# A gated recurrence and a SwiGLU layer on one core: the main path reordered as a list schedule, with smaller first units, narrower weight conversion, on-chip moves and another form of the output product

## The chip, the cores and the metric

The kernel runs on one core of a Trainium2 chip. A core has five engines with a queue each: PE (matrix products; the loads of its stationary operands are listed as PEld), DVE and ACT (elementwise work, ACT also functions from tables that have to be loaded), POOL (elementwise work and DMAs), and SP, which here only starts DMAs. Every queue runs in order. The metric is the device time of one launch in microseconds.

## The reference

For 4 x 8 heads of width D = 48 and 768 steps, a complex state is decayed by a gate and read out by q; the outputs of all heads are one row of 384 features for a feed-forward layer of width 1536.

```python
mag = np.sqrt(a_re * a_re + a_im * a_im)
scale = np.minimum(mag, 0.999) / (mag + 1e-06)
a_re_n, a_im_n = (a_re * scale, a_im * scale)
for t in range(S):
    new_re = ar * S_re - ai * S_im          # ar, ai: row t of a_re_n, a_im_n
    new_im = ar * S_im + ai * S_re
    S_re, S_im = (new_re + kv, new_im)      # kv: outer product of k and v, row t
    y[:, :, t] = np.einsum('bhd,bhde->bhe', q[:, :, t], S_re)
...
xn = x / rms * rms_g                        # x: y as (3072, 384)
silu = g * (1.0 / (1.0 + np.exp(-g)))       # g = xn @ w_gate
return (silu * (xn @ w_val) @ w_out).astype(np.float32)
```

The three weight matrices arrive as float64 and are converted to float32 ("narrowed") in the kernel; [...]this is done on pairs of 32-bit words.

## The kernel before

Time is cut into 24 chunks of C = 128 steps, six to a batch. Inside a chunk the recurrence is a masked product of all pairs of rows plus one product with the state at the chunk's start. For this the decays are turned into a magnitude and an angle per feature and step, accumulated over the chunk, and put into k and q as rotations: every row of k and q becomes a cosine and a sine part.

`fast` (L472) is the path that runs. `general` (L46) stands in the program behind a flag, `bad`, for inputs outside the range that `fast` handles.

- **Gates** (`load_gates` L514, `gates` L560): one call works on a unit of UC = 2 chunks, 768 elements in each of 128 partitions (three blocks j of features by 256 steps). ACT computes squares, inverse roots, arctangent and sines; DVE does products and the running products and sums (scans, L592 and L612). The results go to `rot`, 12 rows of 129 elements per chunk.
- **The move** (L626 to L634): `rot` has (head, feature) on the partitions and the products need the feature alone there. Each chunk is written to `way` in DRAM by one DMA (L629), and read back as `kq` by another (L631), both on SP.
- **Scores** (`scores` L712): 8 heads of k by q into `s_ps`, DVE multiplies by the causal mask into `am` (L723), PE transposes k for the state (L732), ACT copies it to `kt`.
- **Finish** (`finish` L736): the state is updated (L744, DVE); `y_ps` sums, per head, `am` by v (L755) and q by the state (L757), with 48 output columns and the 128 steps on the partitions. ACT squares y and sums its rows (L761), POOL takes the power -1/2 (L765), ACT scales, PE transposes three blocks (L774), DVE multiplies by the norm's weights into `xT` (L775).
- **Feed-forward** (`feed_forward` L780): a group is GC = 3 chunks. For each of 12 blocks of 128 hidden features: gate and value products (L792, 384 moving columns), Silu on ACT (L795), their product on DVE to `hT`; then three output products (L803) and a copy and a store each.
- **Weights** (`load_weights` L682, `narrow` L662): 18 pieces of 768 KB are fetched on SP and narrowed by one ACT operation, two `tensor_scalar` and four two-input DVE operations of 768 elements each. Five fetches are issued at the start, and narrowing goes on between the chunks.

The order is given by Python generators: the loop at the end of `fast` runs `scores(n)` and `finish(n - 1)`, and between their parts pulls pieces of the feed-forward of the group before (`filler`) and of the next unit's gates (`ahead`). In these listings `tt` is DVE's `tensor_tensor`, `stt` its `scalar_tensor_tensor` (both have lines L501 and L504 in the profile).

Of the kernel before, what the change touches and what calls it, by code (L numbers as in the profile page):

```python
# [16 lines left out]
P = 128  # L29
C = 128  # L30
# [440 lines left out]

def fast(tc, ctx, qT, kT, v, a_re, a_im, w_gate, w_val, w_out, rms_g, out, H, bad):  # L472
# [10 lines left out]
    GC = 3  # L483
    NG = N // GC
    GT = GC * C
    UC = 2
    T = UC * C
    NU = N // UC
    L = P // H
    assert NCH % GC == 0 and NCH % UC == 0 and DM % P == 0 and D2 <= P and L * ND == D  # L490

    consts = ctx.enter_context(tc.tile_pool(name="consts", bufs=1))
    prep = ctx.enter_context(tc.tile_pool(name="prep", bufs=1))
    unit = ctx.enter_context(tc.tile_pool(name="unit", bufs=2))
    act = ctx.enter_context(tc.tile_pool(name="act", bufs=2))
    dram = ctx.enter_context(tc.tile_pool(name="dram", bufs=2, space=DRAM))
    ps_a = ctx.enter_context(tc.tile_pool(name="ps_a", bufs=4, space=PSUM))
    ps_g = ctx.enter_context(tc.tile_pool(name="ps_g", bufs=4, space=PSUM))

    def tt(o, x, y, op=ALU.mult):  # L500
        nc.vector.tensor_tensor(out=o, in0=x, in1=y, op=op)  # L501

    def stt(o, x, c, y, op0, op1=ALU.mult, **kw):
        nc.vector.scalar_tensor_tensor(out=o, in0=x, scalar=c, in1=y, op0=op0, op1=op1, **kw)  # L504
# [6 lines left out]
    UN = [dict() for _ in range(NU)]  # L511
    U = [dict() for _ in range(N)]

    def load_gates(u):  # L514
        b, c = divmod(u * UC, NCH)
        t = UN[u]
        for name, ap in (("re", a_re), ("im", a_im)):
            t[name] = prep.tile([P, ND, T], FP32, tag=name, name=name, bufs=2)
            rows = ap[b].rearrange("(h j l) s -> j l h s", j=ND, l=L)
            queue = nc.scalar if u == 0 and name == "im" else nc.sync  # L520
            for j in range(ND):
                queue.dma_start(out=t[name][:, j], in_=rows[j][:, :, c * C:c * C + T])
        for name, ap in (("k", kT), ("q", qT)):
            t[name] = prep.tile([P, ND, T], FP32, tag=name, name=name)
            for i in range(UC):
                nc.sync.dma_start(
                    out=t[name][:, :, i * C:(i + 1) * C],
                    in_=ap[u * UC + i].rearrange("d (h t) -> (d h) t", t=C)
                                      .rearrange("(j p) t -> p j t", p=P))
        for n in range(u * UC, (u + 1) * UC):  # L530
            U[n]["v"] = unit.tile([C, H, D], FP32, tag="v", name="v", bufs=4)
            nc.sync.dma_start(out=U[n]["v"].rearrange("t h d -> t (h d)"),
                              in_=v[n * C:(n + 1) * C, :])
# [3 lines left out]
    rot = consts.tile([P, 4 * ND, UC, C + 1], FP32, name="rot")  # L537
    nc.vector.memset(rot[:, :, :, C:], 0.0)
    load_gates(0)

    zeros = consts.tile([P, T], FP32, name="zeros")
    nc.gpsimd.memset(zeros, 0.0)
    starts = consts.tile([P, ND, UC, C], FP32, name="starts")
    nc.gpsimd.memset(starts, 0.0)
    halfpi = consts.tile([P, 1], FP32, name="halfpi")
    nc.gpsimd.memset(halfpi, PI / 2)
    round_ = consts.tile([P, 1], FP32, name="round_")
    nc.gpsimd.memset(round_, ROUND)
    cap = consts.tile([P, 1], FP32, name="cap")
    nc.gpsimd.memset(cap, CAP)  # L550
    mid = consts.tile([P, 1], FP32, name="mid")
    nc.gpsimd.memset(mid, -(RE_MAX + RE_MIN) / 2)
    width = consts.tile([P, 1], FP32, name="width")
    nc.gpsimd.memset(width, -(RE_MAX - RE_MIN) / 2)
    nc.scalar.activation(out=width, in_=width, func=AF.Abs_reciprocal_sqrt)
    nc.gpsimd.memset(width, -(RE_MAX - RE_MIN) / 2)
    ends = consts.tile([P, NU, ND, UC], FP32, name="ends")
    range_ = consts.tile([P, NU], FP32, name="range_")

    def gates(u):  # L560
        t = UN[u]
        re, im, q, k = (t[x] for x in ("re", "im", "q", "k"))
        act_ = nc.scalar.activation

        s, w, y, r, p = (prep.tile([P, ND, T], FP32, tag=x, name=x)
                         for x in ("s", "w", "y", "r", "p"))
        act_(out=s, in_=re, func=AF.Square)
        act_(out=w, in_=im, func=AF.Square)
        tt(s, s, w, ALU.add)
        act_(out=y, in_=re, func=AF.Abs_reciprocal_sqrt)  # L570
        act_(out=y, in_=y, func=AF.Square)
        act_(out=r, in_=s, func=AF.Abs_reciprocal_sqrt)
        act_(out=w, in_=re, func=AF.Abs, bias=mid)
        act_(out=w, in_=w, func=AF.Relu, bias=width, accum_out=range_[:, u:u + 1])

        tt(im, im, y)
        tt(re, re, y)
        stt(im, re, 2.0, im, ALU.subtract, reverse0=True)
        yield

        tt(w, s, r)
        stt(s, w, -0.5, r, ALU.mult)
        stt(w, s, 1.5, w, ALU.add)

        act_(out=r, in_=r, func=AF.Identity, scale=-CAP * EPS_MAG, bias=cap)
        stt(w, w, EPS_MAG, r, ALU.subtract, ALU.min)

        by_chunk = lambda x: x.rearrange("p j (c t) -> p j c t", t=C)
        wc = by_chunk(w)
        nc.vector.tensor_copy(out=starts[:, :, :, 0:1], in_=wc[:, :, :, 0:1])  # L590
        nc.vector.memset(wc[:, :, :, 0:1], 0.0)
        nc.vector.tensor_tensor_scan(out=flat(p), data0=flat(w),  # L592
                                     data1=starts.rearrange("p j c t -> p (j c t)"),
                                     initial=0.0, op0=ALU.mult, op1=ALU.add)
        nc.vector.tensor_copy(out=ends[:, u], in_=p.rearrange("p j (c t) -> p j c t", t=C)[:, :, :, C - 1])
        nc.vector.tensor_copy(
            out=rot[:, 2 * ND:, :, C].rearrange("p (a j) c -> p a j c", j=ND),
            in_=ends[:, u].unsqueeze(1).to_broadcast([P, 2, ND, UC]))
        yield
        act_(out=r, in_=p, func=AF.Abs_reciprocal_sqrt)  # L600
        act_(out=r, in_=r, func=AF.Square)
        act_(out=im, in_=im, func=AF.Arctan)
        act_(out=im, in_=im, func=AF.Copy, scale=0.5 / PI)

        tt(s, p, r)
        stt(r, s, 2.0, r, ALU.subtract, reverse0=True)
        tt(k, k, r)
        tt(q, q, p)
        yield

        for j in range(ND):
            nc.vector.tensor_tensor_scan(  # L612
                out=re[:, j], data0=im[:, j], data1=zeros, op0=ALU.add, op1=ALU.add,
                initial=UN[u - 1]["turn"][:, j] if u * UC % NCH else 0.0)
        act_(out=w, in_=re, func=AF.Identity, bias=round_)
        stt(im, w, ROUND, re, ALU.subtract, ALU.add, reverse0=True)
        turn = t["turn"] = prep.tile([P, ND, 1], FP32, tag="turn", name="turn", bufs=2)
        nc.vector.tensor_copy(out=turn, in_=im[:, :, T - 1:T])
        act_(out=w, in_=im, func=AF.Abs)
        act_(out=s, in_=im, func=AF.Sin, scale=2 * PI)  # L620
        act_(out=y, in_=w, func=AF.Sin, scale=-2 * PI, bias=halfpi)
        yield
        for i, (x, f) in enumerate(((k, y), (k, s), (q, y), (q, s))):
            tt(rot[:, i * ND:(i + 1) * ND, :, 0:C], by_chunk(x), by_chunk(f))
        yield
        for i in range(UC):  # L626
            n = u * UC + i
            way = dram.tile([4 * DM, C + 1], FP32, tag="way", name="way")
            nc.sync.dma_start(out=way.rearrange("(r p) t -> p r t", p=P), in_=rot[:, :, i])  # L629
            to = unit.tile([D2, 2, H, C + 1], FP32, tag="kq", name="kq", bufs=3)  # L630
            nc.sync.dma_start(out=to.rearrange("d x h t -> d x (h t)"),  # L631
                              in_=way.rearrange("(x d h) t -> d x (h t)", x=2, h=H))
            U[n]["k"], U[n]["q"] = to[:, 0, :, 0:C], to[:, 1, :, 0:C]
            U[n]["decay"] = to[:, 1, :, C:]  # L634
        yield


    ident = consts.tile([P, P], FP32, name="ident")
    make_identity(nc, ident)
    causal = consts.tile([C, C], FP32, name="causal")  # L640
    nc.gpsimd.memset(causal, 1.0)
# [9 lines left out]


    FW = 2 * P
    narrowed = [0]
    EARLY = 3

    def fetch(pool, to, src):
# [262 lines left out]
```

## Time and profile before

| | |
|---|---|
| runs | 889.69, 896.54, 900.56 us; median 896.54 |
| span of the profiled execution | 882.3 us |
| busy: PE, PEld, DVE, ACT, POOL | 773.3, 530.1, 426.8, 356.2, 23.2 us |
| moved by DMA | 81.2 MB, mean 92 GB/s; 293 GB/s in the first 22 us |
| first scores, first gate product, end of the last matmul | 48.8, 122.9, 876.3 us |
| table loads on ACT | 65 of 1.28 us each |
| `way<-rot`, `kq<-way` | 24 DMAs each of 774 KB, median 8.9 and 5.7 us to landing |
| two-input DVE operation of 768, of 384 elements | 0.95, 0.55 us |

A matmul of float32 operands is two records of PE in the profile, each with a weight load of its own. The duration of a record is longer than its distance to the next one, since matmuls overlap in the array; distances of starts say what a matmul costs in a stream. PE's clock is given as a share of full speed.

### The profile page before, as it was taken

To read this page: it belongs to the slowest core of one execution; us is meant where nothing else is said; L and a number is where in the kernel's file an instruction comes from. 1 tells how busy PE (TensorE), PEld (TensorE's weight loads), DVE (VectorE), ACT (ScalarE), POOL (GpSimd) and SP (SyncE) were. 2 spreads that over 40 slices of the span, in tenths; PEclk is the share of its full clock that TensorE was granted. 3 is DMA by queue.
4 is the path that set the end of the run, shared out by engine and by line. 5 is a ranking of instruction groups with operands and counts; after the bars stand their busy time and mean duration, and the time that the engine had idled before them with its cause. 6 is when DMAs were issued, how large, how long until landed. Compare 5 with 4: busy or idle time off the path is not lost.

```text
span 882.3 us, 8797 instructions
## 1 busy us (share of the span) xinstructions
PE 773.3 (88%) x3370; PEld 530.1 (60%) x3370; DVE 426.8 (48%) x654; ACT 356.2 (40%) x520; POOL 23.2 (3%) x42
## 2 busy tenths in 40 slices
PE   0051879888879999999999999999999999999997
PEld 0051857675455566676666667666666767665554
DVE  5978768858978787768785101210121112210110
ACT  6845565643537887676783111111111111110100
POOL 1000000000000000000000000000000000000000
PEclk9995569968989999989999999999999999999999
DMA  8748374852673565482763120112111100000000
GB/s 293 154 110 201 103 169 118 202 138 72 182 186 101 114 154 156 96 189 71 137 162 73 46 63 26 29 45 55 35 29 45 43 21 1 1 9 19 1 1 30
DMA packets 85602, 81.17 MB, mean 92 GB/s; under 512 B 4144, under 2 KB 74800, under 8 KB 85552
## 3 DMA queue, kind: packets, MB, share of 16 engines
q1 hardware_dynamic: 85120, 80.13, 36.3%
q8 instruction: 28, 0.46, 0.2%
q10 hardware_dynamic: 432, 0.39, 0.1%
q14 instruction: 22, 0.18, 0.1%
HBM read 56.77 MB, written 23.74 MB: 91 GB/s over the span
## 4 chain that ended last, share of the span: by engine, by line
PE 80%; DMA 10%; DVE 6%; ACT 2%; issue 1%; SPq 1%; POOL 0%; ACTq 0%; DVEq 0%
PE val_ps L792 20%; PE gate_ps L792 20%; PE out_ps L803 19%; PE s_ps L721 6%; PE y_ps L755 5%; DMA way<-rot 4%; PE y_ps L757 4%; DMA kq<-way 4%; PE state_ps L744 3%; PE kt_ps L732 2%; DVE rot L501 1%; PE xT_ps L774 1%; DMA raw<-in_w_gate_dram 1%; DVE p L592 1%; DVE g L504 1%
## 5 line engine op out<-in xcount | busy, mean ns | idle before, releaser
L792 PE MATMUL gate_ps<-xT,wg 128*128 128x384 f32 x576 | 209.4, 501 | 5.5 <-DVE wg L501 4.8
L792 PE MATMUL val_ps<-xT,wv 128*128 128x384 f32 x576 | 207.7, 497 | 2.2 <-ACT sg L795 2.2
L803 PE MATMUL out_ps<-wo,hT 128*128 128x384 f32 x576 | 192.8, 491 | 0.2
L792 PEld LDWEIGHTS val_ps<-xT,wv 128*128 128x128 f32 x576 | 111.4, 194 | 80.1 <-issue 4.3
L501 DVE TENSOR_TENSOR hT<-val_ps,sg 128x384 f32<-128x384 f32 x96 | 53.3, 555 | 215.8 <-PE val_ps L792 200.4
L792 PEld LDWEIGHTS gate_ps<-xT,wg 128*128 128x128 f32 x576 | 109.0, 196 | 73.7 <-issue 7.9
L803 PEld LDWEIGHTS out_ps<-wo,hT 128*128 128x128 f32 x576 | 108.7, 192 | 71.7 <-issue 1.8
L721 PE MATMUL s_ps<-kq 96*128 96x128 f32 x384 | 57.2, 311 | 77.3 <-DMA kq<-way 77.3
L795 ACT ACTIVATE sg<-gate_ps 128x384 f32<-128x384 f32 x96 | 47.0, 490 | 176.6 <-PE gate_ps L792 176.2
L721 PEld LDWEIGHTS s_ps<-kq 96*128 96x128 f32 x384 | 55.5, 224 | 84.0 <-DMA kq<-way 55.6
L755 PE MATMUL y_ps<-v,am 128*128 128x48 f32 x384 | 76.0, 294 | 0.0
L757 PE MATMUL y_ps<-state,kq 96*128 96x48 f32 x320 | 68.2, 298 | 0.0
L755 PEld LDWEIGHTS y_ps<-v,am 128*128 128x128 f32 x384 | 62.9, 211 | 1.1
L723 DVE TENSOR_TENSOR am<-s_ps,causal 128x512 f32<-128x512 f32 x48 | 32.7, 688 | 51.5 <-PE s_ps L721 51.4
L761 ACT ACTIVATE x<-y_ps 128x384 f32<-128x384 f32 x24 | 11.8, 491 | 110.6 <-PE y_ps L757 101.4
L757 PEld LDWEIGHTS y_ps<-state,kq 96*128 96x128 f32 x320 | 55.1, 215 | 0.3
L808 ACT COPY ot<-out_ps 128x384 f32<-128x384 f32 x24 | 11.4, 475 | 99.3 <-PE out_ps L803 99.3
L765 POOL TENSOR_TENSOR rs<-ssq,mhalf 128x1 f32<-128x1 f32 x24 | 20.8, 867 | 754.7 <-DVE ssq L762 754.7
L733 ACT COPY kt<-kt_ps 128x384 f32<-128x384 f32 x40 | 17.6, 479 | 50.1 <-PE kt_ps L732 50.1
L744 PEld LDWEIGHTS state_ps<-v,kt 128*96 128x96 f32 x320 | 33.0, 179 | 4.4 <-issue 2.4
L744 PE MATMUL state_ps<-v,kt 128*96 128x48 f32 x320 | 32.6, 259 | 0.0
L762 DVE TENSOR_SCALAR ssq<-ssq 128x1 f32<-128x1 f32 x24 | 3.6, 152 | 58.6 <-ACT x L761 58.6
(100 smaller groups left out, 722.6 us busy)
## 6 DMA issues: line engine op xcount, KB each, us to landing
way<-rot SPq DMA_DIRECT2D x24, 774.0 KB, 8.9
kq<-way SPq DMA_DIRECT2D x24, 774.0 KB, 5.7
re<-in_a_re_dram SPq DMA_DIRECT2D x36, 128.0 KB, 2.6
k<-in_k_dram SPq DMA_DIRECT2D x24, 192.0 KB, 2.9
q<-in_q_dram SPq DMA_DIRECT2D x24, 192.0 KB, 3.3
v<-in_v_dram SPq DMA_DIRECT2D x24, 192.0 KB, 2.4
raw<-in_w_gate_dram SPq DMA_DIRECT2D x6, 768.0 KB, 8.2
raw<-in_w_val_dram SPq DMA_DIRECT2D x6, 768.0 KB, 7.0
```

The source lines that it names most:

```text
L501: nc.vector.tensor_tensor(out=o, in0=x, in1=y, op=op)
L721: nc.tensor.matmul(ps[:, h], lhsT=k[:, a * hh + h], rhs=q[:, a * hh + h], start=True, stop=True)
L723: nc.vector.tensor_tensor(out=am[:, a * hh:(a + 1) * hh], in0=ps, op=ALU.mult, in1=causal.unsqueeze(1).to_broadcast([C, hh, C]))
L732: nc.tensor.transpose(ps[:, h], k[:, a * hh + h], ident[0:D2, 0:D2])
L733: nc.scalar.copy(out=kt[:, a * hh:(a + 1) * hh], in_=ps)
L744: nc.tensor.matmul(ps[:, h], lhsT=u["kt"][:, h], rhs=vv[:, h], start=True, stop=True)
L755: nc.tensor.matmul(ps[:, h], lhsT=am[:, h], rhs=vv[:, h], start=True, stop=prev is None)
L757: nc.tensor.matmul(ps[:, h], lhsT=q[:, h], rhs=prev[:, h], start=False, stop=True)
L765: nc.gpsimd.tensor_tensor(out=rs, in0=ssq, in1=mhalf, op=ALU.pow)
L792: nc.tensor.matmul(p_, lhsT=w_[:, d, fs], rhs=xT[:, d], start=d == 0, stop=d == ND - 1)
L795: nc.scalar.activation(out=sg, in_=gp, func=AF.Silu)
L803: nc.tensor.matmul(ps, lhsT=hT[:, f, i * C:(i + 1) * C], rhs=wo[:, f], start=f == 0, stop=f == NF - 1)
```

## The change

The whole body of `fast` is written anew.

- **Order.** Every instruction is first noted in a `Flow` object with its engine, an assumed duration and its operands; dependences follow from overlapping boxes of memory. `schedule` gives each a due time, counted back from those of the feed-forward, and places them one after the other on the engines, on each the ready one that is due first; a change of ACT's table set counts as 4 us. The instructions are then issued in the order of that plan, and the framework adds the waits. All buffers are fixed ("rooms"), the eight PSUM banks too: four for the feed-forward, four for the rest.
- **Units.** Gates run on units of one, one, and then two chunks. Feed-forward groups hold 1, 1, 2 and then 4 chunks, with up to 512 moving columns.
- **Gates.** The magnitude's running product is taken of its square, in one scan with two products per 128 steps; one product goes to POOL. DVE has fewer instructions of full width and more small ones.
- **Move.** Six DMAs of 128 KB for each chunk go from `rot` to `kq` directly, on SP.
- **Weights.** Fetches are issued on POOL. Narrowing is one ACT, two DVE and one POOL operation. Fetched words first lie in the rooms of `wo` and `hT`, that are not in use yet. The test for numbers too small for float32 is taken out of narrowing: `look` fetches all 18 pieces a second time on SP into one room, and DVE takes a minimum of each.
- **y.** It is computed transposed, features on the partitions. Each block of 32 features is a product of 32 stationary columns (values, padded to 80 per pair of heads, or states) and 128 moving columns (`am` or q), written to 32 of the 128 output partitions. Four such column groups take turns. The transposes to `xT` go; the mean square is a product with a column of ones, its inverse root is spread over the partitions by another product, and DVE multiplies it in.

The assumed durations lie in the helpers (`tt`, `stt`, `act`, `mms` and the like), which replace the direct calls. Cut to its core:

```diff
+class Flow:
+    SYNC = 0.12
+    TABLES = {"silu": ("S",), "sin": ("S", "T"), "arctan": ("T",), "rsqrt": ("A",)}
...
+    def dates(self):
...
+            for u in users[op["i"]]:
+                x = self.ops[u]
+                stretch = 1.0 if x["eng"] == "PE" else 1.35
+                due = min(due, x["due"] - x["dur"] * stretch - (x["land"] or 0.0) - 0.2)
...
+    def schedule(self):
...
+                key = o["due"]
+                if o["table"] and table not in self.TABLES[o["table"]]:
+                    key += self.switch
+                if pick is None or key < pick[0]:
+                    pick = (key, o)
...
+    def issue(self):
+        for op in sorted(self.ops, key=lambda o: o["order"]):
+            for fn, args, kw in op["calls"]:
+                fn(*args, **kw)
...
-    UC = 2
...
+    UNITS = [[0], [1]] + [[n, n + 1] for n in range(2, N, 2)]
+    GROUPS = [[0], [1], [2, 3]] + [list(range(n, n + 4)) for n in range(4, N, 4)]
...
-        nc.scalar.activation(out=to, in_=as_to(hi.bitcast(FP32)), func=AF.Square)
-        stt(as_to(g.bitcast(FP32)), to, (1.125 * 2.0 ** -15) ** 2, as_to(hi.bitcast(FP32)), ALU.is_ge)
-        nc.vector.tensor_scalar(out=t, in0=g, scalar1=3, scalar2=0x3FFFFFFF,
-                                op0=ALU.logical_shift_left, op1=ALU.bitwise_and)
-        stt(t, g, -2 ** 30, t, ALU.bitwise_and, ALU.bitwise_or)
-        nc.vector.tensor_scalar(out=g, in0=t, scalar1=-2 ** 23, scalar2=None, op0=ALU.bitwise_and)
-        stt(to, as_to(lo.bitcast(U32)), 2.0 ** -52, as_to(g.bitcast(FP32)), ALU.mult)
-        tt(to, as_to(t.bitcast(FP32)), to, ALU.add)
+    def narrow(i):
...
+        lo, hi = fetch(i, place(i), "POOL")
+        as_to = lambda x: x.rearrange("p (c f) -> p c f", f=n)
+        t = to.bitcast(I32)
+        act(lo, lo.bitcast(U32), AF.Copy, scale=2.0 ** -29)
+        ts(t, as_to(hi), 3, 0x3FFFFFFF, ALU.logical_shift_left, ALU.bitwise_and)
+        stt(t, as_to(hi), -2 ** 30, t, ALU.bitwise_and, ALU.bitwise_or)
+        tt(t, t, as_to(lo), ALU.add, eng="POOL")
+    def look(i):
...
+        lo, hi = fetch(i, raws[0], "SP")
+        hf = hi.bitcast(FP32)
+        add("DVE", [(nc.vector.tensor_reduce, (),
+                     dict(out=small[:, i:i + 1], in_=hf, axis=mybir.AxisListType.X, op=ALU.min,
+                          apply_absolute_value=True))], 1.0, [hf], [small[:, i:i + 1]])
...
+        for j in range(ND):
+            for i in range(nt):
+                cs = slice(i * C, (i + 1) * C)
+                scan(t4[:, j, cs], t2[:, j, cs], t1[:, j, cs], 1.0, ALU.mult, ALU.mult)
...
+        tt(q, q, t4, eng="POOL")
...
+        for a, f in enumerate((t5, t3)):
+            tt(f, f, t2)
+            for i, n_ in enumerate(ns):
+                cs = slice(i * C, (i + 1) * C)
+                for o, x in ((0, k), (C, q)):
+                    tt(rots[n_ % 2][:, a * ND:(a + 1) * ND, o:o + C], x[:, :, cs], f[:, :, cs])
+        for n_ in ns:
+            for r in range(2 * ND):
+                dma(kqs[n_ % 3][r * L:(r + 1) * L], rots[n_ % 2][:, r], "SP")
...
+        for i in range(4 * ND):
+            j, c = divmod(i, 4)
+            m, r = divmod(i, 3)
+            o = yT[c * BLK:(c + 1) * BLK, j]
+            part = [(2 * m, 0)] if r == 0 else [(2 * m, 1), (2 * m + 1, 2)] if r == 1 else [(2 * m + 1, 3)]
+            todo = []
+            for h, g in part:
+                todo.append((vf[:, m, g * BLK:(g + 1) * BLK], am[:, h]))
+                if not first:
+                    todo.append((sf[:, m, g * BLK:(g + 1) * BLK], q[:, h]))
+            for x, (l_, r_) in enumerate(todo):
+                lines[c].append((o, l_, r_, x == 0, x == len(todo) - 1))
+        order = [lines[c][i] for i in range(len(lines[0])) for c in range(4)]
+        mms(order, len(order) * mm_time(C) / 4 * 1.1 + 0.15)
...
+        act(sq, yT, AF.Square)
+        tt(yg, yT, gcol.unsqueeze(2).to_broadcast([P, ND, C]))
+        tt(sq[:, 0], sq[:, 0], sq[:, 1], ALU.add)
+        tt(sq[:, 0], sq[:, 0], sq[:, 2], ALU.add)
...
+        mms([(col, sq[:, 0], ones, True, True)], 0.25)
+        ts(ssv[n % 2], col, 1.0 / DM, EPS_RMS, ALU.mult, ALU.add)
...
+        mms([(wide, rss[n % 2].to_broadcast([P, P]), ident, True, True)], 0.25)
...
+        tt(xT[:, :, i * C:(i + 1) * C], yg, wide.unsqueeze(1).to_broadcast([P, ND, C]))
...
+    flow.schedule()
+    with tc.manual_schedule():
+        flow.issue()
```

## The prediction

> **What bounds it now.** I read three views in this order. First the busy time by stage (columns: stage, its length, then busy time and number of instructions of PE, PEld, DVE, ACT and POOL, granted clock, DMA share, GB/s):
>
> ```profile
> 0.00:44.00 44.00, 0.00 (x0) 0.00 (x0) 34.10 (x47) 32.44 (x39) 2.36 (x18) 1.00 0.80 224
> 44.00:132.00 88.00, 52.05 (x253) 47.01 (x253) 65.88 (x97) 47.87 (x64) 4.08 (x3) 0.65 0.61 146
> 132.00:286.00 154.00, 131.06 (x579) 91.75 (x580) 123.48 (x184) 81.02 (x112) 4.53 (x5) 0.89 0.54 142
> 286.00:790.00 504.00, 504.00 (x2272) 341.10 (x2271) 196.50 (x315) 186.10 (x289) 12.20 (x16) 0.99 0.29 70
> ```
>
> From 286 us on PE never rests, at full clock: that stage is bound by PE's own instructions. Before it PE is idle or at a reduced clock, while DVE is busy about three quarters of the time (34.1 of 44, 65.9 of 88, 123.5 of 154). Second, what PE waited for between 44 and 286 us (total, times, longest):
>
> ```profile
> PE s_ps L721 <- DMA kq<-way: 77.3, 5, 48.8
> PE xT_ps L774 <- ACT xn L767: 15.4, 6, 6.4
> PE gate_ps L792 <- DVE wg L501: 4.8, 2, 3.1
> ```
>
> The scores wait for the rotated rows, which come through DRAM behind DVE's gates. Third, PE's timeline, for what one pass (a float32 matmul is two records) costs at full clock (start, duration):
>
> ```profile
> 133.17 2.02 PE L721 MATMUL s_ps<-kq 96*128 96x128 f32 x16 [1.89 <-DMA kq<-way]
> 135.03 0.82 PE L732 MATMUL kt_ps<-ident,kq 96*128 96x96 f32 x8
> 135.69 1.48 PE L792 MATMUL val_ps<-xT,wv 128*128 128x384 f32 x4
> 137.00 1.48 PE L744 MATMUL state_ps<-v,kt 128*96 128x48 f32 x16
> 138.32 0.39 PE L755 MATMUL y_ps<-v,am 128*128 128x48 f32 x2
> ...
> 141.90 2.17 PE L792 MATMUL gate_ps<-xT,wg 128*128 128x384 f32 x6
> 143.90 2.10 PE L792 MATMUL val_ps<-xT,wv 128*128 128x384 f32 x6
> 145.84 2.10 PE L792 MATMUL gate_ps<-xT,wg 128*128 128x384 f32 x6
> ```
>
> Differences of starts are the true prices: gate and value 1.94/6 = 0.323 us a record, s 1.86/16 = 0.116, kt 0.66/8 = 0.083, state 1.32/16 = 0.083, the chunk's 32 y records 3.58/32 = 0.112, and by the same reading xT 0.107. Times the counts: 1728 x 0.323 = 558; 384 x 0.116 = 44.5; 704 x 0.112 = 79; 320 x 0.083 = 26.6; 160 x 0.083 = 13.3; 72 x 0.107 = 7.7. **PE's own work is 729 us.** The span is 882.3: 6 us lie after the last matmul (876.3), about 4 are small gaps after 286 us, and **some 143 us are lost in the first 286 us**, to idleness and to the clock.
>
> **What the Trainium skill says.** (1) "TensorE: Matmul & The Clock Gate", LDWEIGHTS: a weight load costs its columns / 1.2 ns whatever the rows. The trace agrees: 128 columns give 107, y takes 112; 96 give 80, state takes 83. So y, with 48 moving columns, pays for its weights. (2) The same page, Part 3: matmuls in different column groups run side by side; three measured 2.38 times. No row of this trace shows one. (3) "TensorEngine Tiling (Array Packing)", Key Properties: changing the tiling mode drains the engine; no price, not in this trace. (4) "SBUF — State Buffer", two separate sides: a GpSimd operation and a VectorE operation on two SBUF inputs exclude each other for a whole instruction. Here POOL only runs 0.87 us powers, so this trace cannot show it. A price from "GPSIMD Engine Reference", 3.1: an elementwise sum is 1.96 times slower than on DVE; estimate for 768 elements 1.96 x 0.95 = 1.9 us.
>
> **The change part by part: PE.** FF moves the same columns (groups of 1, 1, 2, then 4 chunks). The two single groups have 128-column records bound by the weight load: 288 x (0.112 - 0.108) = +1. Scores, state and kt stay. The xT transposes go (-7.7); the column sum and the row broadcast come: 24 x 4 records x 0.11 = +10.6. y is the doubtful term. Before, 8 heads give 32 records with 128 weight columns. Now 16 head parts give 64 records, with 32 weight columns (27 ns) and 128 moving columns (107 ns, a third of 0.323). Records: 24 x 32 + 20 x 32 = 1408. If four groups truly overlap, 0.028 us each = 39. But a matmul's two records hit the same column group one after the other and the queue is in order, so perhaps only the second of one overlaps the first of the next: 0.055 = 77. Without overlap 0.112 = 158. I take 0.045 = 63, that is -16. Drains: 48 mode changes, from 0 to one record's latency (0.273, median duration of xT's) = 0 to 13; I take 6. Sum 729 + 1 - 7.7 + 10.6 - 16 + 6 = **723**.
>
> **DVE.** Before, a two-chunk gate unit has 17 instructions at 0.95, a scan at 1.74, three at 0.72 and small ones: 20.8. Now nine at 0.95, one at 0.55, six 128-wide scans (0.45, from the two scan sizes), three at 0.74, eight 384-wide products at 0.55, small 0.65: 19. A one-chunk unit, at 0.55 an instruction, is about 10.5. Narrowing a piece falls from 4.9 (four 0.95, two 0.55) to 1.5, 61 us less over 18; its product moves to POOL (1.9 each) and ACT keeps one 0.9. Attention rises from 3.2 to 4.3 a chunk (yg 0.55, two sums 0.28). So chunks 0 to 3, their FF products and all weights cost 2 x 10.5 + 19 + 27 + 4 x 4.3 + 4 = 88 us, where two units and the weights alone took 2 x 20.8 + 88 = 130. The second look at the weights (18 reductions of about 0.95) is not due and lies beside FF; DVE was busy 39% of the long stage. If that cover failed it would cost 17.
>
> **ACT.** 65 table loads of 1.28 now; the new order charges for each, but Silu, sine, arctangent and root still alternate. After the start it had 318 us of slack in 504, so I cost it at nothing; in the start it counts in the chain: one chunk is 15 instructions of about 0.5 and up to four loads, 13 us.
>
> **Queues.** SP loses 24 writes to `way` and 24 reads (7.2 and 6.7 us in the chain, first chunk), and gains 144 moves of 128 KB: six issues at 0.56 (k's, 1.12 for two) and some 2.6 to land (re, the same size) = 6 us instead of 14. SP also gets 18 second fetches. Each waits for the one room, with the next loads and moves behind it; one stuck fetch would delay scores, but SP issues only about 0.6 x 390 = 234 us, so I cost it at nothing. POOL gets the 18 fetches; a fetch that waits for its room holds back what is queued behind it: the sums that free the next rooms, the v copies and the powers that xT waits for. POOL's load, 18 x 1.9 + 12 x 1.9 + 24 x 1.6 = 96 us, is spread, but up to 45 of it falls in the start and can shut out DVE.
>
> **The start.** First FF: loads about 5, one-chunk chain 13 on ACT and some 8 of DVE not beside it, move 6, attention 6: 38 us, where gate's first record came at 122.9. Then DVE needs its 88, and the DMA 14.2 MB of weights plus six chunks of 1.8 MB, 25 MB at 224 to 293 GB/s (the first stages) = 85 to 110. So PE is fed fully from about 95 us, having done FF of one chunk (23), part of the second (10) and four attentions (22) = 55: 40 lost, and 15 for half clock: **55 lost for 143**. Bounds: 35 if nothing collides, 85 if POOL excludes DVE for 30 us more. What is late next is the weights.
>
> **Sum.** 723 + 55 + 4 + 6 = 788 for the profiled execution of 882.3. The median of the runs is 896.54, 14.2 above that span; the same added gives **802**.
>
> **Rivals.** A, the above: y at 39 to 77 and start at 35 to 85 give 744 to 832, runs 758 to 846. 68 in 100. B, the start stays bound: POOL, the DMA and ACT's tables take DVE's gain, 120 us lost: 723 + 120 + 10 = 853, run 867. For it: DMA already at 0.80 in the first stage. Against: 61 us less narrowing. 14. C, column groups do not overlap: y 158, 723 + 95 + 65 = 883, run 897. 7. D, slower: each column-group record waits for the one ahead to leave the array, at the 0.275 us that a record lasts from end to end (median of s). y costs 1408 x 0.275 = 387, 788 + 324 = 1112, run 1126. It decides from the point where y eats the gain: 63 + 94 + 18 (2%) = 175, or 0.124 us a record. For it: small records already start no closer than 0.083. Against: all of them overlap their neighbours now. 11, with smaller prices of the same mechanism.
>
> **Chances.** About 2% (18 us) is what a measurement of this kernel tells from no change: below 879 is faster, above 914 slower. A and B give 82 faster, C 7 the same, D 11 slower. The range 764 to 872 holds most of A and of B; D and C are left out.
>
> **What would show it.** A first gate record near 38 us and PE full from 95 confirm the start; DVE or POOL holding full slices beyond that speaks for B. y's start-to-start near 0.03, 0.055 or 0.112 us decides the main term. kq moves should land in about 3 us. The forecast is wrong if PE shows gaps after 100 us (a fixed order that waits), or if y's records do not overlap.

## The result and the profile after

| | before | after |
|---|---|---|
| runs | 879.97 to 900.56 us, median 893.12 of 4 | 800.34 to 804.05 us, median 801.18 of 4 |
| span of the profiled execution | 882.3 us | 802.3 us |
| busy: PE, DVE, ACT, POOL | 773.3, 426.8, 356.2, 23.2 us | 717.3, 427.5, 350.1, 115.8 us |
| first scores, first gate product | 48.8, 122.9 us | 45.6, 90.4 us |

The ratio is 0.908 (95% interval 0.900 to 0.916): the kernel is faster by 92 us. The forecast was 802. That the total came out nearly exact is luck: two of its terms were off by 25 and 40 us in opposite directions, and a third, of 14 us, should not have been in it. The stages first, in the columns of the stages before (stage, length, busy time and number of instructions of PE, PEld, DVE, ACT, POOL, clock, DMA share, GB/s):

```profile
0.00:160.00 160.00, 84.43 (x710) 74.15 (x711) 135.36 (x191) 99.11 (x133) 72.99 (x69) 0.96 0.72 178
160.00:200.00 40.00, 39.69 (x279) 35.14 (x279) 34.46 (x60) 30.87 (x38) 4.73 (x3) 1.00 0.56 129
200.00:286.00 86.00, 85.91 (x456) 49.64 (x455) 66.71 (x123) 62.78 (x78) 8.45 (x9) 1.00 0.66 145
286.00:790.00 504.00, 501.29 (x2640) 288.29 (x2639) 190.95 (x349) 156.81 (x217) 29.60 (x35) 1.00 0.29 59
```

PE now rests hardly at all from 160 us on (2.7 us in the last 504), and at full clock. What is lost lies before 160 us, where PE is busy for 84 of 160 us and DVE for 135. PE's own starts show where it waits there, and for what (start, duration, operation, in brackets the idle time before it and what ended it):

```profile
45.57 3.78 PE L595 MATMUL bank<-kq 96*128 96x128 f32 x16 [45.57 <-DMA kq<-rot]
...
60.37 0.80 PE L595 MATMUL bank<-ident,rs 128*128 128x128 f32 x2 [4.42 <-POOL rs L595]
72.84 2.47 PE L595 MATMUL bank<-kq 96*128 96x128 f32 x10 [11.68 <-DMA kq<-rot]
...
90.38 0.85 PE L595 MATMUL bank<-xT,wg 128*128 128x128 f32 x3
```

Chunk 0 has its scores at 45.6 and its norm at 60.4, yet the next work on PE is chunk 1's scores at 72.8, and the first feed-forward product comes at 90.4. In the steady part the same view shows the new form of y:

```profile
544.78 0.43 PE L595 MATMUL bank<-am,ve 128*32 128x128 f32 x8
545.02 0.40 PE L595 MATMUL bank<-kq,state 96*32 96x128 f32 x8
545.24 0.40 PE L595 MATMUL bank<-am,ve 128*32 128x128 f32 x8
...
546.34 0.41 PE L595 MATMUL bank<-kq,state 96*32 96x128 f32 x8
546.68 2.05 PE L595 MATMUL bank<-kq 96*128 96x128 f32 x16
```

Eight records (four matmuls of float32, one in each column group) start every 0.22 us: about 0.028 us a record. A chunk's 64 records take from 544.78 to 546.68, that is 1.9 us, where its 32 longer records took 3.58 before.

### The profile page after: what moved, and what is told of

It is laid out like the page before. It is cut to its first block, busy times and chain, and to the rows that moved or that the text cites. A ratio compares the mean times of both kernels' runs of the same rounds, so it can differ in the third digit from the quotient of the medians.

```text
span 802.3 us, 10571 instructions
## 1 busy us (share of the span) xinstructions
PE 717.3 (89%) x4098; PEld 450.4 (56%) x4098; DVE 427.5 (53%) x721; ACT 350.1 (44%) x465; POOL 115.8 (14%) x116
## 5 line engine op out<-in xcount | busy, mean ns | idle before, releaser
L595 PE MATMUL bank<-xT,wg 128*128 128x512 f32 (+2 forms) x576 | 202.0, 496 | 1.2 <-DVE xT L595 0.6
L595 PE MATMUL bank<-wo,hT 128*128 128x384 f32 x576 | 197.2, 490 | 4.7 <-POOL wo L595 4.6
L595 PE MATMUL bank<-xT,wv 128*128 128x512 f32 (+2 forms) x576 | 198.0, 487 | 2.0 <-DVE hT L595 1.3
L595 PEld LDWEIGHTS bank<-xT,wg 128*128 128x128 f32 x576 | 101.9, 200 | 87.7 <-issue 83.0
L595 PEld LDWEIGHTS bank<-xT,wv 128*128 128x128 f32 x576 | 98.5, 190 | 90.5 <-issue 85.4
L595 DVE TENSOR_TENSOR hT<-bank,sg 128x512 f32<-128x512 f32 x72 | 49.7, 690 | 183.5 <-PE bank L595 180.2
L595 PEld LDWEIGHTS bank<-wo,hT 128*128 128x128 f32 x576 | 105.4, 190 | 70.5 <-POOL wo L595 6.5
L595 PE MATMUL bank<-kq 96*128 96x128 f32 x384 | 53.7, 292 | 58.0 <-DMA kq<-rot 57.2
L595 PEld LDWEIGHTS bank<-kq 96*128 96x128 f32 x384 | 49.6, 203 | 61.8 <-DMA kq<-rot 45.6
L595 ACT ACTIVATE t<-t 128x768 f32<-128x768 f32 (+3 forms) x65 | 51.1, 791 | 19.8 <-DVE t L595 19.0
L595 DVE TENSOR_TENSOR t<-t,t 128x768 f32<-128x768 f32 (+1 forms) x39 | 39.5, 1018 | 14.2 <-ACT t L595 14.2
```

Source lines behind the costliest of these rows:

```text
L595: fn(*args, **kw)
```

## Experiments

Every experiment is made from the changed kernel, so its time is to be held against 801.2 us.

**1. The column groups one after the other.** The order of y's products, within the same code:

```diff
-        order = [lines[c][i] for i in range(len(lines[0])) for c in range(4)]
+        order = [lines[c][i] for c in range(4) for i in range(len(lines[0]))]
```

> The 64 y records of a chunk stand in another order: all of column group 0, then 1, 2, 3, instead of in turns. Nothing else moves. Theory (four groups run side by side, which is why y costs 0.0277 us a record in the changed kernel): without turns each record waits for the one ahead in its own columns, 0.107 us, the time of 128 moving columns; 1408 x 0.079 = 112 us more, about 913. Rival (the saving comes from the small weight load of 32 columns, 27 ns, not from overlap): records stay at about 0.028 to 0.03 us and the time stays at 801.

879.2 us (877.7 and 880.8), ratio to before 0.985 (0.974 to 0.997): 78 us slower than the change. PE's timeline of this kernel, the y of one chunk in the steady part:

```profile
503.26 0.41 PE L595 MATMUL bank<-am,ve 128*32 128x128 f32 x2
...
503.94 0.38 PE L595 MATMUL bank<-kq,state 96*32 96x128 f32 x2
504.16 0.38 PE L595 MATMUL bank<-am,ve 128*32 128x128 f32 x2
504.38 0.38 PE L595 MATMUL bank<-kq,state 96*32 96x128 f32 x2
504.60 0.41 PE L595 MATMUL bank<-am,ve 128*32 128x128 f32 x4
...
509.19 0.49 PE L595 MATMUL bank<-ident,rs 128*128 128x128 f32 x2
```

Two records in 0.22 us instead of eight: products that hit the same column group follow each other at 0.11 us a record. The line at 504.60 shows four records in that time: where one group's list ends and the next group's begins, neighbours overlap even here. The 64 records take 5.9 us (503.26 to 509.19). For the 20 chunks of 64 records that is 20 x 4.0 = 80 us more, and the run showed 78 (the four chunks of 32 records are not in this sum). The expected 112 had every record at 0.107 us and no overlap where two groups meet. Taking turns over the four groups is what makes the new y pay: a chunk's records took 3.58 us in the old form, take 5.9 group by group and 1.9 in turns. Written in the other order, the whole change would have gained only 1.5%.

**2. POOL's sums and DVE.** The last of narrowing's operations is a sum on POOL. One kernel leaves it out (its weights lack their last three bits), a second puts it on DVE, both with the order of the change's plan:

```diff
-        tt(t, t, as_to(lo), ALU.add, eng="POOL")
+        tt(t, t, as_to(lo), ALU.add, eng="POOL")["calls"] = []
```

```diff
-        tt(t, t, as_to(lo), ALU.add, eng="POOL")
+        tt(t, t, as_to(lo), ALU.add, eng="POOL")["calls"] = [
+            (nc.vector.tensor_tensor, (), dict(out=t, in0=t, in1=as_to(lo), op=ALU.bitwise_or))]
```

> Same plan and order, but the 18 sums on POOL (2.06 us each) that add the last three bits to the narrowed weights are left out. Theory (POOL and DVE exclude each other while both read SBUF, and the start is bound by DVE): two-input DVE operations before 155 us fall back to their lone durations (0.95 us for 768 elements instead of 1.4, 0.55 for 384 instead of 0.92 for rot<-k), some 20 to 25 us of DVE time; PE is full about 20 us earlier and the run ends at 780 to 788. Rival (the start is bound by the DMA or by PE's fixed order, and DVE's longer durations lie in slack): 797 to 802.

> Same plan and order, but the 18 sums run on DVE (as a bitwise OR of the same words) instead of POOL. Costs DVE 18 x 0.95 = 17 us in a start where it is full, and takes away the exclusion. Theory (exclusion costs DVE 20 to 25 us): the two nearly cancel, 793 to 801. Rival (exclusion costs nothing that counts): 17 us of DVE come on top, 812 to 818.

796.8 us without the sums, 795.7 with them on DVE, where they are work of DVE's own and still cost less than on POOL. How the sums hurt DVE is seen in two timelines of the changed kernel (POOL's, then DVE's):

```profile
64.35 4.62 POOL L595 TENSOR_TENSOR wg<-wg,hT 128x768 int32<-128x768 int32 x1 [3.31 <-ACT t L595]
...
94.31 2.45 POOL L595 TENSOR_TENSOR wg<-wg,raw 128x768 int32<-128x768 int32 x1 [4.58 <-issue]
```

```profile
67.30 2.48 DVE L595 SCALAR_TENSOR_TENSOR im<-t,im 128x768 f32<-128x768 f32 x1
...
94.97 1.82 DVE L595 TENSOR_TENSOR ends<-t,t 128x3 f32<-128x3 f32 x1
...
96.90 0.16 DVE L595 TENSOR_TENSOR ends<-t,t 128x3 f32<-128x3 f32 x1
```

An operation of three elements takes 1.82 us, and ends at 96.79, when the sum on POOL ends (94.31 + 2.45 = 96.76). The same operation takes 0.16 when it comes next, at 96.90. The other way round, the sum that starts at 64.35 takes 4.62 while DVE is at work, and a DVE operation after it 2.48 instead of 0.95. "SBUF — State Buffer", two separate sides, in the Trainium skill says just this: one of the two holds the port pair for a whole instruction and the other is blocked. Two groups of DVE's operations before 155 us (busy time, mean ns) show it, here in the changed kernel:

```profile
L595 DVE TENSOR_TENSOR rot<-k,t 128x384 f32<-128x384 f32 x12 | 10.7, 919 | 0.1
L595 DVE TENSOR_TENSOR t<-t,t 128x768 f32<-128x768 f32 x7 | 9.9, 1423 | 0.0
```

and in the kernel without sums:

```profile
L595 DVE TENSOR_TENSOR t<-t,t 128x768 f32<-128x768 f32 x7 | 6.6, 951 | 0.3 <-ACT t L595 0.3
L595 DVE TENSOR_TENSOR rot<-k,t 128x384 f32<-128x384 f32 x12 | 6.3, 554 | 0.1
```

Over the whole execution DVE's busy time falls from 427.5 to 401.0 us: 26 us of DVE's time in the start were waiting, shown as work. That only 4.4 of them reached the end is the puzzle of the start. The run ended just below the rival's range (797 to 802) and far from the theory's (780 to 788). DVE's timeline in the kernel without sums says what came instead:

```profile
51.51 0.69 DVE L595 TENSOR_TENSOR am<-bank,causal 128x512 f32<-128x512 f32 x1 [12.13 <-PE bank L595]
```

DVE, whose order is fixed, waits 12 us for the scores of chunk 0, whose rows land at 49.4 us.

**3. The weights' bytes.** Moves of `kq` take 5.2 us to land (median of all; 8.1 in the first 90 us), where 2.6 were forecast, and the DMA engines are busy at 0.93 in the first 40 us. One kernel holds back the weights from the fifth piece on until chunk 0's rows have landed (`held` is a copy on POOL of one column of its `kq`):

```diff
+        op = dma(raw3, src, eng)
+        if eng == "POOL" and i >= 4:
+            op["deps"].add(held["i"])
```

> Weight pieces from the fifth on are fetched only after chunk 0's moves have landed (a one-element copy on POOL reads the moved rows, and the fetches are planned behind it). In the changed kernel the first moves are issued at 31.9 to 36.5 us and the scores start at 45.6, with the DMA busy 0.90 to 0.96 in the first 40 us. Theory D (weight fetches delay the gates' loads and the moves, and this holds up the start): first scores at about 36, chunk 1's before 68, run at 788 to 797. Rival W (the weights are what is late in the start; holding them back delays the first output products): first scores still come early, but PE is full 5 to 15 us later, run at 805 to 815.

809.8 us, 8.6 more, as rival W had it. Chunk 0's scores come at 37.1 instead of 45.6, but the first output product at 122.2 instead of 110.4: the weights lose more than chunk 0 wins. So I took the bytes away instead, once with the sums in place and once without (the output is then not that of the reference):

```diff
         op = dma(raw3, src, eng)
+        if eng == "POOL":
+            op["calls"] = [(nc.gpsimd.dma_start, (), dict(out=raw3[:, 0], in_=src[:, 0]))]
...
+    for x in wrooms + raws + hrooms:
+        fill(x, 0, eng="DVE", due=0.0)
```

> Of each weight piece the first fetch brings only the first row of its two or three (a third of gate's and value's bytes, half of out's); the rest of the room is zero, so the output is not that of the reference. 8.6 MB less in the start, all narrowing work and the plan stay but for 7 fills of 0.8 us on an idle DVE in the first 8 us. Theory D (DVE's total of work sets the end of the start, the bytes lie beside it): moves land sooner and the first gate comes earlier, but PE is full hardly sooner: 797 to 802. Theory W (the weights' arrival sets it: 8.6 MB at some 300 GB/s is 29 us): 775 to 790.

> As the run with a third of the weights' bytes, and POOL's sums of the last bits left out too (26 us of DVE's time, alone worth 4.5 us). If bytes and DVE bound the start one after the other, each hiding the other, the two together give far more than 4.5 plus what the bytes alone give: 770 to 782. If DVE alone bounds it, 793 to 797. If a third thing does (the fixed order, ACT's chain), 790 to 796 with DVE idle and DMA low before 140 us.

795.3 us with a third of the bytes, between what the two theories had for it, so neither D nor W holds alone. With both taken away: **776.1 us** (774.7 to 777.7), in the range of the case in which each bound hides the other. The four kernels make a table of two by two:

| | sums on POOL | no sums | gain |
|---|---|---|---|
| all bytes | 801.2 | 796.8 | 4.4 |
| a third to a half of the bytes | 795.3 | 776.1 | 19.2 |
| gain | 5.9 | 20.7 | 25.1 both |

The stages show why, here 40 to 100 us and 100 to 160 us. First the change itself:

```profile
40.00:100.00 60.00, 31.75 (x250) 29.57 (x251) 53.10 (x71) 34.71 (x48) 28.43 (x19) 0.91 0.50 123
100.00:160.00 60.00, 52.68 (x463) 44.58 (x462) 58.78 (x86) 42.33 (x53) 25.91 (x15) 0.97 0.81 169
```

without the sums:

```profile
40.00:100.00 60.00, 28.83 (x255) 27.40 (x256) 39.89 (x67) 32.20 (x42) 9.19 (x11) 0.77 0.55 130
100.00:160.00 60.00, 56.77 (x491) 48.50 (x490) 52.21 (x92) 47.76 (x60) 8.71 (x7) 1.00 0.93 198
```

with a third of the bytes:

```profile
40.00:100.00 60.00, 36.98 (x304) 34.38 (x304) 53.82 (x75) 36.42 (x47) 24.77 (x20) 0.97 0.40 91
100.00:160.00 60.00, 54.57 (x453) 46.45 (x454) 57.29 (x87) 40.55 (x51) 17.80 (x13) 0.94 0.72 138
```

and with both:

```profile
40.00:100.00 60.00, 42.71 (x402) 40.18 (x402) 52.15 (x88) 43.58 (x55) 8.62 (x11) 0.86 0.53 105
100.00:160.00 60.00, 60.00 (x466) 51.09 (x465) 51.84 (x93) 46.25 (x59) 6.97 (x6) 1.00 0.74 161
```

Without sums DVE has 20 us of idleness in the first of these stages (39.9 of 60), and DMA is near full in the second (0.93). With few bytes it is the other way: DMA falls to 0.40 and 0.72 (0.50 and 0.81 in the change), and DVE is as full as before (53.8 and 57.3). Only with both gone does PE get its work, 402 instructions instead of 250 between 40 and 100 us, with the first gate product at 72.7 instead of 90.4 us. The sums on POOL and the weights' bytes are thus two limits of nearly the same length, each of which hides the other. How the sums act is shown only in part. They stretch DVE's operations, but they also stand on POOL's queue, where the next fetch into a room waits for the sum before it: with few bytes, the last fetch of the output weights is issued at 107.4 us with sums and at 90.8 without. A run with few bytes and the sums on DVE would tell the two apart, and was not made.

**4. The first units.** Units and groups of two from the start, as one part of the change undone:

```diff
-    UNITS = [[0], [1]] + [[n, n + 1] for n in range(2, N, 2)]
-    GROUPS = [[0], [1], [2, 3]] + [list(range(n, n + 4)) for n in range(4, N, 4)]
+    UNITS = [[n, n + 1] for n in range(0, N, 2)]
+    GROUPS = [[0, 1], [2, 3]] + [list(range(n, n + 4)) for n in range(4, N, 4)]
...
```

> The first two chunks form one unit and one group again (units of two throughout, groups of 2, 2 and then 4 chunks), planned anew. Theory (small first units bring the first scores forward): the first gates work on 768 elements, scores come about 8 us later than 45.6 and the first FF cannot start on chunk 0 alone; 806 to 815. Rival (the weights and DVE's total set the start, not the first chunk): DVE's share falls a little with wider instructions (19 instead of 21 us for the two chunks) and the N = 128 records go; 797 to 803.

795.5 us, below both ranges. The first scores come later (53.4 for 45.6), the first gate product sooner (80.8 for 90.4), the first output product later (125.8 for 110.4). One-chunk units and groups bring the first chunk earlier, and yet cost 5.7 us in all; which part of them costs it was not taken apart.

**5. The order.** In the planner, blocks of a weight with a stride are noted as one box from the first to the last byte, so the plan believes that the first gate product needs all six pieces of `wg`. One kernel notes exact boxes:

```diff
-        np_, hi = 1, lo + size
+        np_, inner = 1, []
...
-        return name, p0, p0 + np_, lo, hi
+        return [(name, p0, p0 + np_, l, h) for l, h in runs]
```

> The planner's boxes are made exact: a block of weight columns over three row blocks is noted as three stretches, not as one that reaches over its neighbours. In the changed kernel the plan believes that the first gate products need all six wg pieces, and puts chunk 1's attention ahead of them on PE: first gate at 90.4 us though xT of chunk 0 is there at 62.3. Theory A (this misplaced order costs PE's idle time): first gate near 62, up to 17 us of PE work moves into the gaps before 90, run at 786 to 794. Theory B (the start is bound by DVE and the weights, PE's gaps only change place): 798 to 803.

801.6 us, no change, although the first gate product comes at 56.0 instead of 90.4. The gaps only change place: in the first 200 us PE waits less for the moves and the norm than in the change (52 us for 68), and more for POOL's sums of the weights (9 for 5) and for DVE (13 for 2). The other test gives the schedule up altogether:

```diff
-        for op in sorted(self.ops, key=lambda o: o["order"]):
+        for op in self.ops:
```

> All parts of the change stay, but each engine issues its operations in the order in which the program notes them, not in the order of the list schedule: a chunk's whole attention, then the next chunk's, and a group's FF after the attention of its last chunk. Theory (the list schedule is what keeps PE free of gaps: in noted order PE waits in each chunk for the mask on DVE, and in each group for the norm, some 10 us a chunk with nothing between, and all 18 narrowings stand on DVE ahead of chunk 0): 801 + 24 x 10 = 1040, 960 to 1120. Rival (the semaphores and buffers leave enough slack that order hardly matters): under 880.

1647.3 us, twice the change's time and far beyond what I expected. The waits of PE in this kernel (total, times, longest):

```profile
PE bank L595 <- DMA kq<-rot: 554.1, 13, 132.4
PE bank L595 <- POOL ve L595: 180.6, 12, 140.5
```

I had priced gaps inside an attention, 10 us a chunk. But the gates of a unit stand, in noted order, behind the feed-forward ahead of it on DVE and ACT too, so PE waits for a whole chain of gates and moves at each of 13 units (554 / 13 = 43 us), and once 140 us on a copy that stands on POOL behind all 18 fetches and sums. So the gates have to run ahead of PE, and this order does not let them; beside such gaps PE's clock has a mean of 0.76 (0.99 in the change). What the list schedule gains over the interleaving of the kernel before, which also ran the gates ahead, was not tried.

**6. Two edits that were costed.** The second look at the weights left out (its fetches and reductions), and the move made through DRAM again:

```diff
-        dma(raw3, src, eng)
+        if eng == "POOL":
+            dma(raw3, src, eng)
+        else:
+            dma(raw3, src, eng)["calls"] = []
...
-        add("DVE", [(nc.vector.tensor_reduce, (),
...
+        add("DVE", [(nc.vector.memset, (small[:, i:i + 1], 1.0), {})], 1.0, [hf], [small[:, i:i + 1]])
```

```diff
-                dma(kqs[n_ % 3][r * L:(r + 1) * L], rots[n_ % 2][:, r], "SP")
+            dma(way.rearrange("(r p) t -> p r t", p=P), rots[n_ % 2], "SP")
+            dma(kqs[n_ % 3].rearrange("d h t -> d (h t)"), way.rearrange("(d h) t -> d (h t)", h=H), "SP")
...
```

> Same plan; the second fetch of the 18 pieces and the 18 reductions (0.946 us each on DVE) are left out, so the test for too small weights is not made (its flags are set to 1). Theory (they lie beside PE's work: one reduction before 155 us, the others where DVE is under half busy): 799 to 802, no change. Rival (the one room and the fetches in SP's queue hold up loads and moves: SP waited 48.6 us on these reductions): 790 to 797.

> The move goes through DRAM again: one write of 789 KB and one read per chunk instead of six direct moves, planned anew. Theory (the move is in the chain of the first chunks only): 24 x 1.6 MB of DMA instead of 0.8, and some 7 to 10 us more from rotated rows to scores for chunks 0 and 1, 806 to 820; steady state unchanged. Rival (the direct moves are as slow, since each goes to 16 partitions only: 5.2 us median to landing): 799 to 804.

803.5 us without the second look, no less than with it: it costs nothing. 808.9 us with the way through DRAM: 7.7 us more, with chunk 0's scores at 53.9 instead of 45.6.

**7. What is worth keeping.** The units of two and the sum on DVE, together, a kernel that computes all of the reference:

> Two chunks for the first units and groups, and the last three bits added on DVE as a bitwise or, together. Alone they gave 795.5 and 795.7 us against 801.2. Theory (both take work off the same full DVE of the start, by different instructions, so they add): 801.2 - 5.7 - 5.5 = 790, 787 to 793. Rival (once DVE is relieved by the one, the arrival of the weights is the limit and the other buys nothing): 794 to 797.

**789.8 us** (789.2 to 791.2), ratio to before 0.890 (0.882 to 0.899). The gains add (11.4 for 5.7 and 5.5).

## Why the prediction was right in its total, and where not

- **y, mis-sized.** I took 0.045 us a record (63 us) because a matmul's two records would hit one column group in turn. Measured is 0.028, 1408 records are 39 us, my lower bound: the four groups overlap fully. With the drains (what the eight steps of 0.22 us leave of a chunk's y, and the gap ahead of it, is about 0.2 us a chunk, 5 us, forecast 6), PE's own work is 723 - 24 - 1 = 698. "TensorE: Matmul & The Clock Gate", Part 3, with 2.38 for three groups and 512 moving columns, stood on the careful side here: four gave 0.11 / 0.028, about 4.
- **The start, wrong.** "55 lost for 143", bounds 35 to 85. With PE's own work 698, some 3 us of gaps and 6 after the last matmul, the start lost 802.3 - 698 - 9 = **95 us**, beyond the upper bound. The first gate product was forecast at 38 us and came at 90.4 (by experiment 5 this landmark alone is worth nothing), PE was to be full from 95 and was so from about 160. PE's gaps after 100 us, named ahead as a sign against the forecast, are there: 7 us of them until 160. The step that failed is "Then DVE needs its 88, and the DMA ... 85 to 110", taken side by side as if neither slowed the other. DVE's 88 became about 119: 26 of blocking beside POOL, which I had named ("up to 45 of it falls in the start") but priced only in the bound, and some 5 because the `tensor_scalar` of the `wg` and `wv` pieces took 0.94 us, not 0.55. The rest of the 135 us that DVE was busy is gates and attention of later chunks. And the moves landed in 8.1 us, not 2.6, in the first 90 us; the weights' bytes are a part of that, since a third of them left 5.7. Of the 40 us missed, sums and bytes together account for at most 25, by experiment 3 (at most, because the forecast had counted the bytes too), and the one-chunk units and groups for some 6; those add only as far as they were tried, and what is left was not taken apart. ACT's table loads rose from 65 to 78, which was costed at nothing; after 160 us PE's waits for ACT come to under 1 us, and in the start it was not tried alone.
- **Where the gain lies.** Of the 80 us between the two profiled spans, PE's own work gives some 31 (729 to 698) and the start some 48 (143 to 95). Experiment 1 shows what the 31 hang on. What shortened the start was tried only for the move; the new narrowing and the new gates were not undone alone.
- **Added by mistake, 14.2 us.** The median of before lay that far above its profiled span. I added it as if it went with every kernel. But a run of the change lies 1.7 us above its own span (804.05 and 802.3), and launches of before in these runs lie between 880 and 905: the difference was mostly the spread of before, not a cost. The sum to compare is 788 with 802.3.
- **Right, in part by luck.** The moves on chip were to save 8 us (6 for 14) and saved 7.7, with both ends off: from the first issue to the scores the direct moves took 13.7 us (31.9 to 45.6), and the way through DRAM 19.0 in the changed kernel (34.9 to 53.9). The second look at nothing. Full PE and full clock after the start. Rival D is excluded by 0.028 us a record; rival C is what experiment 1 made, 879 for its 897. Rival B, the bound start, was the better half of the truth (95 lost, between its 120 and my 55), with y making up for it.
- **A reading that left something out.** "The trace agrees" on weight loads holds for y and the state; kt's records also load 128 columns and follow each other at 0.083 us. The sum does not hang on it.

## What to carry to other kernels

Small products that fill only 32 columns are cheap if products of different column groups are issued in turns (0.028 us a record here), and not otherwise (0.11). Work moved from a full engine to a helper is only free if the helper doesn't hold up the full one: compare the mean durations of the full engine's operations, beside the helper and away from it. When taking one suspect away changes little, take two away together before clearing either.

## What was not expected of the hardware

- Four column groups overlap fully for float32 products of 32 stationary and 128 moving columns: 0.028 us a record in turns, 0.11 within one group.
- A `tensor_scalar` of 768 int32 elements takes 0.94 us for pieces of `wg` and `wv`, as long as a two-input operation of 768 (0.95), and 0.55 for those of `wo` (one of the six, beside POOL, 2.25). All of them read every second word; the first write three blocks of 256 columns, the last one unbroken stretch. That this decides was not tried alone.

```profile
L595 DVE TENSOR_SCALAR wg<-wo 128x768 int32<-128x768 int32 x3 | 2.8, 937 | 0.0
L595 DVE TENSOR_SCALAR wo<-raw 128x768 int32<-128x768 int32 x1 | 0.5, 545 | 0.0
```

- POOL's sum of 768 such elements takes 1.8 to 2.5 us, and up to 4.6 while DVE works; a DVE operation of three elements beside it took 1.82 instead of 0.16.
- Moves of 128 KB within the chip take 5.2 us to land (median). Loads of that size took 2.6 in the kernel before, and 3.5 to 4.6 in the changed one.
